# Routing search in four steps instead of six, one running sum instead of two, a new table of planner numbers and a branch hint

## The chip, the cores and the metric

The kernel runs on one core of a Trainium2 chip. The time is the device time in microseconds of one execution; three executions were timed before the change, and one more was profiled.

## The reference, cut to what matters

Attention over 8 batches, 8 heads, 576 tokens and 64 features keeps the 32 largest scores of each row. Its output, as 4608 tokens of 512 features, goes through 8 experts. Each token gets one expert, in the order of the logits, and no expert takes more than 576 tokens:

```
logits = x @ w_gate
flat = logits.flatten()
order = np.argsort(-flat)
...
for idx in order:
    tok, e = (int(idx) // E, int(idx) % E)
    if assigned[tok] >= 0 or counts[e] >= cap:
        continue
    assigned[tok] = e
...
    h = np.maximum(x[mask] @ w1[e], 0.0)
    out[mask] = h @ w2[e]
```

The inputs are fixed by their seed.

## The kernel before

The first part is attention. It writes `x` to DRAM and the logits `L` (128 partitions, 36 columns of 8 experts) to SBUF. The change leaves it alone. The second part, `moe`, runs the experts one after the other, in the order in which they fill up. For place p in that order there are five pieces.

`route` finds the expert that fills next. Each free token bids its largest logit for its best expert. In each of 6 steps VectorE compares all bids with 32 thresholds (`g`, L847) and TensorE counts, for each threshold and expert, the bids that lie above (`pc`, L851 for p = 0, L853 for the others). The highest threshold that some expert still fills 576 times becomes the lower end of the next step, with a spacing 32 times finer. For p = 0 a step has 36 small count matmuls; for p = 1 to 6 it has 9, and then two more matmuls (`tot`, L864, and `quart`, L867) with VectorE operations between them. The last expert needs no search. After the last step VectorE makes two masks: `M1` (L889) has the bids above the upper end of the last interval, `M2` (L890) has those within it. Each gets a running sum (`cs`, L900 and L901) and a sum over partitions on TensorE (L905 to L907), and they are joined to positions `pos` and a selection `sel` that is cut at 576 tokens.

`enlist` turns positions into a list of token numbers `idx` (L925 to L964). `weigh` reads the expert's number `ei` into a register of the SyncE queue (SP, L970), loads `w1` and `w2` in four pieces of 1 MB (`wr`, four buffers, L978), and splits each number into two float16 parts, on ScalarE (`w1h`, `w2h`, L990) and VectorE (`w1l`, `w2l`, L998). `bring` gathers the tokens by indirect DMAs of GpSimd (`xg`, L1020), five for each expert. For p = 0 TensorE turns them (L1033) and ScalarE and VectorE write the parts of `xT` (L1034, L1035); for the others VectorE and ScalarE make the parts first (L1043, L1046) and a transposing DMA of the SP queue turns them (L1047). `ffn` multiplies: 192 matmuls of `w1` (L1065), a ReLU in two parts `hh` and `hl` (L1084, L1085), 120 matmuls of `w2` (L1099, L1102), and a scatter of five tiles `ob` to the output (L1109 to L1114). The first four groups of p = 0 are cut, so that 128 columns can begin when the first gathered tile is there.

The order of all this isn't written out. `Plan` takes each operation with its engine, its cost, its predecessors and a due time, and simulates the engines: of what can begin soonest it emits that with the lowest due time. The table `O` in `moe` holds the numbers by which due times of the pieces are shifted, and windows for each engine. The emitted order is each engine's program, and an engine runs its program strictly in order. `stay` (L769) puts dummy matmuls into TensorE's gaps ahead of the first expert.

`verdict` checks that attention was exact and writes flags. At the end `redo` reads them on every engine (L629) and branches (L630): if one is set, faulty heads are computed again and `moe` is run again. Behind the branch stands the last scatter (L1175), of the last tile of the last expert.

Of the kernel before, what the change touches and what calls it, by code (L numbers as in the profile page):

```python
# [9 lines left out]
F32 = mybir.dt.float32  # L10
# [614 lines left out]
def redo(tc,q,k,v,w_gate,x,L,flags,again):  # L625
# [3 lines left out]
    any_=nc.values_load(flags[0:1,32:33],min_val=0,max_val=32)  # L629
    with tc.If(any_>0):  # L630
# [72 lines left out]
MT=32; MSTEPS=6  # L703
# [42 lines left out]
def moe(tc, K, L, x, w1, w2, out, tail, marks=None):  # L746
# [4 lines left out]
    T=MT; STEPS=MSTEPS; BIG=1e30; SX=128.0; SW=128.0; OSC=1.0/(SX*SW*SW)  # L751
    with ExitStack() as ctx:
# [6 lines left out]
        O=dict(WL1=-67.48, WL2=33.053, R1=216.021, XL=85.087, FA=-155.406, RT=5997.879, TE=0.633, TN=-42.68, WT=61.707, XT=21.675, RD=-5966.067, GL=2.3, W_V=0.109, W_A=0.0071, W_G=1000.0, W_P=0.0363, W_D=874040.4423, WD0=8.825, WD1=33.963, RA=16.129, WT0=-69.551, TE0=-175.381, XT0=-143.142, VD=228.308)  # L759
# [22 lines left out]
        U=cp.tile([128,NT],F32,name="U"); V.memset(U,1.0)  # L782
        stp=cp.tile([128,STEPS],F32,name="stp"); lo0=cp.tile([128,1],F32,name="lo0")
# [37 lines left out]
        def route(p,c):  # L821
# [13 lines left out]
            if p<E-1:  # L835
                pcs=3 if p==0 else GP; n=NT//pcs
                D_["lo"]=lo0; lowop=None
                for s in range(STEPS):
# [17 lines left out]
                    if p:  # L856
# [9 lines left out]
                        c.add("V",.07,lambda: V.tensor_scalar(o("ok",128,E,dt=BF16),D_["pn"][:,:E],float(CAP),-1.0/T,op0=ALU.is_ge,op1=ALU.add),k=0)  # L866
                        c.add("P",.04,lambda: P.matmul(D_["pn"][:,16:16+E],quart,D_["ok"],start=True,stop=True,skip_group_check=True))  # L867
# [19 lines left out]
                c.add("V",.3,high)  # L887
                c.add("V",.07,lambda: V.tensor_scalar(o("mem",128,NT),D_["ce"],D_["win"],None,op0=ALU.is_equal))
                c.add("V",.17,lambda: V.scalar_tensor_tensor(o("M1",128,NT),D_["v"],D_["hi"],D_["mem"],op0=ALU.is_ge,op1=ALU.mult))  # L889
                c.add("V",.17,lambda: V.scalar_tensor_tensor(o("M2",128,NT),D_["v"],D_["lo"],D_["mem"],op0=ALU.is_ge,op1=ALU.mult))  # L890
                c.add("V",.1,lambda: V.tensor_tensor(D_["M2"],D_["M2"],D_["M1"],op=ALU.subtract))
            else:
# [3 lines left out]
                def rest(): V.memset(o("M1",128,NT),0.0); V.tensor_copy(o("M2",128,NT),U)  # L896
                c.add("V",.2,rest)
            e["D"]=D_; e["ei"]=ei

            c.add("V",.17,lambda: V.tensor_tensor_scan(o("cs",128,2,NT)[:,0,:],onesf[:,:NT],D_["M1"],0.0,op0=ALU.mult,op1=ALU.add))  # L900
            c.add("V",.17,lambda: V.tensor_tensor_scan(D_["cs"][:,1,:],onesf[:,:NT],D_["M2"],0.0,op0=ALU.mult,op1=ALU.add))  # L901
            c.add("V",.07,lambda: V.tensor_copy(o("tot",128,2,dt=BF16),D_["cs"][:,:,NT-1]))
            def bases():
                pb=D_["pb"]=new(ps,[128,512],F32,"pc",1); tot=D_["tot"]
                P.matmul(pb[:,0:1],tri,tot[:,0:1],start=True,stop=True)  # L905
                P.matmul(pb[:,1:2],tri,tot[:,1:2],start=True,stop=False)
                P.matmul(pb[:,1:2],onesb,tot[:,0:1],start=False,stop=True)  # L907
            c.add("P",.08,bases)
            c.add("V",.07,lambda: V.tensor_copy(o("bs",128,2),D_["pb"][:,0:2]))
            c.add("V",.17,lambda: V.scalar_tensor_tensor(o("pos",128,NT),D_["cs"][:,0,:],D_["bs"][:,0:1],D_["M1"],op0=ALU.add,op1=ALU.mult))  # L910
            c.add("V",.17,lambda: V.scalar_tensor_tensor(o("p2",128,NT),D_["cs"][:,1,:],D_["bs"][:,1:2],D_["M2"],op0=ALU.add,op1=ALU.mult))
            c.add("V",.1,lambda: V.tensor_tensor(D_["pos"],D_["pos"],D_["p2"],op=ALU.add))
            c.add("V",.07,lambda: V.tensor_scalar(o("sel",128,NT),D_["pos"],0.5,None,op0=ALU.is_ge))
            e["sel"]=c.add("V",.1,lambda: V.scalar_tensor_tensor(D_["sel"],D_["pos"],float(CAP),D_["sel"],op0=ALU.is_le,op1=ALU.mult))
# [6 lines left out]
        def enlist(p,c):  # L921
# [3 lines left out]
            c.add("V",.07,lambda: V.tensor_scalar(o("pi",128,NT,dt=I32),D_["pos"],-1.0,None,op0=ALU.add))  # L925
# [8 lines left out]
            c.add("V",.15,lambda: V.tensor_tensor(tks,tk,D_["sel"].unsqueeze(1).to_broadcast([128,2,NT]),op=ALU.mult))  # L934
            last=[]
            for (u0,u1) in ((0,20),(20,36)):
                js=slice(u0,u1); n=u1-u0
# [265 lines left out]
```

## Time and profile before

| | |
|---|---|
| three timed executions | 1335.47 to 1340.48 us, median 1337.67 us |
| the profiled execution | 1336.32 us, of which the span of instructions is 1334.6 us |
| TensorE (PE) busy | 1228.7 us, 92% |
| VectorE (DVE) busy | 1143.0 us, 86% |
| ScalarE (ACT) busy | 953.5 us, 71% |
| GpSimd (POOL) busy | 831.8 us, 62% |
| granted TensorE clock | 0.979 of full speed in the mean |

Times in views of the trace are microseconds from the start of the span. Attention ends at about 868 us; the experts fill the rest. A busy share is a mean over stages that differ, so the stages of the second part are read one by one.

### The profile page before, as it was taken

The page shows a single profiled execution, that of the slowest core. Times are in us where ns is not written, and L with a number is a line of the kernel's source. Part 1 is how long each engine was busy: PE and PEld are TensorE (multiplying, and loading weights), DVE is VectorE, ACT ScalarE, POOL GpSimd, SP SyncE. Part 2 cuts the span into 40 slices and gives each one's busy share as a digit, 9 for nine tenths or more (in the row PEclk, how much of TensorE's full clock was granted, in tenths as well). Part 3 has the DMA queues.
Part 4 walks back from the last instruction along what each step waited for, and adds up shares of the span by engine and source line. Part 5 has one row for each costly group of instructions (what it writes and reads, how often), then busy time and mean ns, then how long its engine had stood idle before and what let it go on. Part 6 is the DMA issues. An engine that isn't in the chain of part 4 may idle for free.

```text
span 1334.6 us, 44588 instructions
## 1 busy us (share of the span) xinstructions
PE 1228.7 (92%) x16596; PEld 928.8 (70%) x16597; DVE 1143.0 (86%) x5729; ACT 953.5 (71%) x2241; POOL 831.8 (62%) x1219
## 2 busy tenths in 40 slices
PE   7999999999999999999999999838999999999996
PEld 6777777777777777777777777737565575665662
DVE  7989999999999899999999999579999898887520
ACT  4989999999999899999999999604433433433420
POOL 3888988988998899889889988701303203215101
PEclk9999999999999999999999999958999999999998
DMA  5544654654545545555554563013544644555601
GB/s 107 102 82 84 137 102 78 130 102 94 120 97 100 118 85 100 102 116 94 105 126 85 97 135 74 23 64 124 191 169 107 196 155 117 170 173 159 179 21 38
DMA packets 317973, 148.67 MB, mean 111 GB/s; under 512 B 283441, under 2 KB 299825, under 8 KB 316721
## 3 DMA queue, kind: packets, MB, share of 16 engines
q1 hardware_dynamic: 311408, 126.55, 42.4%
q0 software_dynamic: 5888, 18.88, 4.6%
q8 instruction: 132, 2.16, 0.7%
q14 instruction: 97, 0.79, 0.2%
q10 hardware_dynamic: 448, 0.30, 0.1%
HBM read 71.34 MB, written 18.87 MB: 68 GB/s over the span
## 4 chain that ended last, share of the span: by engine, by line
PE 29%; POOL 20%; ACT 18%; DVE 16%; issue 11%; DMA 5%; SPq 0%; POOLq 0%; ACTq 0%; another core or an unknown queue 0%; DVEq 0%
PE ph L1065 12%; POOL elm L456 10%; PE ph L1099 9%; DVE cd L371 6%; ACT w L385 6%; ACT F L450 4%; DMA Q<-nq 3%; POOL ehm L453 3%; ACT nq L309 2%; DVE st L398 2%; ACT r L403 2%; POOL e4l L509 2%; PE ph L1102 1%; PE s L367 1%; ACT st L381 1%
## 5 line engine op out<-in xcount | busy, mean ns | idle before, releaser
L371 DVE MAX8 cd<-s 128x8 f32<-128x96 f32 x1728 | 348.9, 248 | 10.8 <-PE s L367 10.3
L456 POOL TENSOR_TENSOR elm<-F,ehm 128x512 f16<-128x512 f32 x256 | 292.5, 1159 | 0.0
L398 DVE MAX8 st<-s 128x8 f32<-128x584 f32 x288 | 219.0, 770 | 9.6 <-PE s L388 5.9
L367 PE MATMUL s<-K,Q 128*128 128x192 f16 (+3 forms) x1280 | 197.5, 287 | 27.6 <-ACT r L403 9.0
L385 ACT ACTIVATE w<-s,st 128x576 uint16<-128x576 f32 x288 | 214.0, 743 | 8.3
L403 ACT ACTIVATE r<-s,st 128x576 bf16<-128x576 f32 x288 | 211.7, 746 | 0.6 <-DVE st L398 0.5
L1065 PE MATMUL ph<-xT,w1h 128*128 128x288 f16 (+2 forms) x1056 | 193.5, 283 | 0.4 <-DMA xT<-xs 0.4
L446 PE MATMUL pt<-Q,K 66*128 66x128 f16 (+1 forms) x1280 | 185.4, 215 | 0.9 <-DMA Q<-nq 0.8
L445 PE MATMUL pt<-Q,K 128*128 128x128 f16 (+1 forms) x1280 | 185.1, 214 | 0.0
L453 POOL TENSOR_SCALAR ehm<-F 128x512 f16<-128x512 f32 x256 | 156.4, 620 | 45.9 <-ACT F L450 45.9
L1114 POOL DMA_INDIRECT out_dram<-ob,idx x39 | 42.2, 1081 | 224.7 <-ACT ob L1109 203.7
L388 PE MATMUL s<-w,off 128*128 128x384 f16 x576 | 149.8, 284 | 20.3 <-ACT w L385 18.8
L450 ACT ACTIVATE F<-pt 128x512 f32<-128x512 f32 x256 | 153.3, 599 | 7.3 <-PE pt L446 4.1
L367 PEld LDWEIGHTS <-Q 128*128 128x128 f16 (+1 forms) x1280 | 99.9, 101 | 72.6 <-issue 61.8
L1065 PE MATMUL ph<-xT,w1l 128*128 128x288 f16 (+2 forms) x528 | 148.8, 283 | 0.0
L1020 POOL DMA_INDIRECT xg<-x,idx x40 | 44.2, 1106 | 144.4 <-DVE idx L964 60.3
L1084 ACT ACTIVATE hh<-ph 128x288 f16<-128x288 f32 x128 | 52.3, 410 | 113.3 <-PE ph L1065 96.7
L542 PE MATMUL pv<-vh,ehm 128*128 128x65 f16 x1024 | 119.8, 195 | 0.3 <-ACT F L450 0.3
L542 PE MATMUL pv<-vh,elm 128*128 128x65 f16 x1024 | 119.7, 193 | 0.4 <-POOL elm L456 0.4
L542 PE MATMUL pv<-vl,ehm 128*128 128x65 f16 x1024 | 119.9, 193 | 0.0
L446 PEld LDWEIGHTS <-K 66*128 66x128 f16 x1280 | 117.5, 98 | 2.1
L445 PEld LDWEIGHTS <-K 128*128 128x128 f16 x1280 | 117.0, 98 | 2.2 <-issue 1.8
(294 smaller groups left out, 3529.7 us busy)
## 6 DMA issues: line engine op xcount, KB each, us to landing
wr<-in_moe_w_dram SPq DMA_DIRECT2D x32, 1024.0 KB
kn<-in_k_dram SPq DMA_DIRECT2D x64, 128.0 KB
vt<-in_v_dram SPq DMA_DIRECT2D x64, 128.0 KB
x<-xb SPq DMA_DIRECT2D x8, 1024.0 KB
qn<-in_q_dram SPq DMA_DIRECT2D x62, 128.0 KB
Q<-nq SPq DMA_TRANSPOSE x160
kn<-in_k_dram SPq DMA_DIRECT2D x64, 16.0 KB
K<-nk SPq DMA_TRANSPOSE x64
```

Of the source, the lines that this page charges most:

```text
L367: x=T.matmul(s_ps[rows,S0+a:S0+b_],P[Q][:,qc],P[K][:,h*576+a:h*576+b_],start=(Q=="Q1"),stop=(Q=="Q2"))
L371: x=V.max(D["cd"][:,c*8:c*8+8],D["s"][:,S0+CW*c:S0+CW*(c+1)])
L385: A.activation(D["w"],D["s"][:,S0:S0+576],AF.Sign,bias=P["st"][:,i,32:33],scale=(1+2.0**-21),accum_out=acc[:,col])
L398: def next8(): V.max(P["st"][:,i,24:32],D["s"][:,S0-8:S0+576])
L403: A.activation(r,D["s"][:,S0:S0+576],AF.Relu,bias=P["st"][:,i,31:32],scale=-1.0)
L445: T.matmul(o,K2[:,kb:kb+128],Q1[:,qc],start=False,stop=False,skip_group_check=True)
L446: T.matmul(o,K3[0:66,kb:kb+128],Q2[0:66,qc],start=False,stop=(c==3 and h==sub[-1][0]),skip_group_check=True)
L450: A.activation(D["E"],D["pt"],AF.Exp,scale=ESC)
L453: G.tensor_scalar(D["eh"],D["E"],1.0,0.0,op0=ALU.mult,op1=ALU.add)
L456: G.tensor_tensor(el,D["E"],D["eh"],op=ALU.subtract); P["e"][i]=(D["eh"],el)
L542: for m_ in (range(N-3) if part==0 else range(N-3,N)): T.matmul(out,seq[m_][0],seq[m_][1],start=(m_==0),stop=(m_==N-1))
L1065: P.matmul(B["ph"][:,lo-c0:hi-c0],a[:,c,fs],xT[:,b+c,lo:hi],start=(i==0),stop=(i==11),skip_group_check=True)
```

## The change

`moe` takes a second number of steps: its first run (the one with `marks`) searches in 4 steps, the run inside `redo` in 6 as before. In the first run there is one mask, `sel`: the bids of the winning expert above the lower end. It gets one running sum, which begins at -1 so that it gives positions from 0 on, one sum over partitions, and one product to the integer positions `pi`; the cut at 576 is gone. In its place the last step keeps how many bids each threshold has above 575 (`ov`), sums over experts (`os`) and notes whether some threshold has a sum of exactly one (`one`), which is so when one expert has exactly 576 there and no other that many. `verdict` counts these notes and sets a further flag for each search that had none; then `redo` runs `moe` again with 6 steps.

For the planner, the load of a weight piece now costs 5.2 on the queue instead of 0.45, and all numbers of `O` are new. The product of token numbers and selection (`tks`) is due before the sums. At the end, the flags are read into registers before the last tile's `ob` is written, with a prefetch hint for the branch on ScalarE and GpSimd, and that write has to wait for the flags in the plan.

```diff
-MT=32; MSTEPS=6
+MT=32; MSTEPS=(6,4)
...
-    T=MT; STEPS=MSTEPS; BIG=1e30; SX=128.0; SW=128.0; OSC=1.0/(SX*SW*SW)
+    T=MT; STEPS=MSTEPS[1 if marks else 0]; BIG=1e30; SX=128.0; SW=128.0; OSC=1.0/(SX*SW*SW)
...
-        O=dict(WL1=-67.48, WL2=33.053, R1=216.021, XL=85.087, FA=-155.406, RT=5997.879, TE=0.633, TN=-42.68, WT=61.707, XT=21.675, RD=-5966.067, GL=2.3, W_V=0.109, W_A=0.0071, W_G=1000.0, W_P=0.0363, W_D=874040.4423, WD0=8.825, WD1=33.963, RA=16.129, WT0=-69.551, TE0=-175.381, XT0=-143.142, VD=228.308)
+        O=dict(FA=-381.864, GL=2.3, R1=211.263, RA=127.04, RD=-5914.06, RT=5987.22, TE=66.9612, TE0=-353.618, TN=-183.558, VD=361.245, WD0=43.2348, WD1=-15.6663, WL1=-283.997, WL2=71.1213, WT=-36.2651, WT0=18.9534, W_A=0.0415342, W_D=874040, W_G=1000, W_P=0.00439945, W_V=0.0355924, XL=25.6353, XT=45.8383, XT0=1.12987)
...
+                        if marks and s==STEPS-1: over=plan.at(c.t+.01,lambda: V.tensor_scalar(o("ov",128,E)[:T],D_["pn"][:T,:E],1.0-CAP,0.0,op0=ALU.add,op1=ALU.max),c.pre,e="V",d=.07,k=0)
...
-                def high():
-                    V.tensor_scalar(o("t1",128,1),D_["mx"],1.0,None,op0=ALU.add)
-                    V.scalar_tensor_tensor(o("hi",128,1),D_["t1"],stp[:,STEPS-1:STEPS],D_["lo_"],op0=ALU.mult,op1=ALU.add)
...
-                c.add("V",.17,lambda: V.scalar_tensor_tensor(o("M1",128,NT),D_["v"],D_["hi"],D_["mem"],op0=ALU.is_ge,op1=ALU.mult))
-                c.add("V",.17,lambda: V.scalar_tensor_tensor(o("M2",128,NT),D_["v"],D_["lo"],D_["mem"],op0=ALU.is_ge,op1=ALU.mult))
-                c.add("V",.1,lambda: V.tensor_tensor(D_["M2"],D_["M2"],D_["M1"],op=ALU.subtract))
+                if marks:
+                    r_=T if p==0 else 128
+                    n_=plan.at(c.t+2.0,lambda: V.tensor_reduce(o("os",128,1)[:r_],D_["ov"][:r_],axis=AX.X,op=ALU.add),[over],e="V",d=.07,k=0)
+                    e["one"]=plan.at(c.t+2.1,lambda: V.tensor_scalar(one[:r_,p:p+1],D_["os"][:r_],1.0,None,op0=ALU.is_equal),[n_],e="V",d=.07,k=0)
+                    c.add("V",.07,lambda: V.tensor_scalar(o("mem",128,NT),D_["ce"],D_["win"],None,op0=ALU.is_equal))
+                    e["sel"]=c.add("V",.17,lambda: V.scalar_tensor_tensor(o("sel",128,NT),D_["v"],D_["lo"],D_["mem"],op0=ALU.is_ge,op1=ALU.mult))
...
+            if marks:
+                c.add("V",.17,lambda: V.tensor_tensor_scan(o("cs",128,NT),onesf[:,:NT],D_["sel"],-1.0,op0=ALU.mult,op1=ALU.add))
+                c.add("V",.07,lambda: V.tensor_scalar(o("tot",128,1,dt=BF16),D_["cs"][:,NT-1:NT],1.0,None,op0=ALU.add))
+                def bases():
+                    D_["pb"]=new(ps,[128,512],F32,"pc",1); P.matmul(D_["pb"][:,0:1],tri,D_["tot"],start=True,stop=True)
+                c.add("P",.05,bases)
+                c.add("V",.07,lambda: V.tensor_copy(o("bs",128,1),D_["pb"][:,0:1]))
+                e["pos"]=c.add("V",.17,lambda: V.scalar_tensor_tensor(o("pi",128,NT,dt=I32),D_["cs"],D_["bs"],D_["sel"],op0=ALU.add,op1=ALU.mult))
...
-                ops.append(plan.at(c.t+.05*k,load,c.pre,take="wr",e="D",d=.45,late=2.0+3.0*(k+1),order=ops[-1:]))
+                ops.append(plan.at(c.t+.05*k,load,c.pre,take="wr",e="D",d=5.2,late=2.0,order=ops[-1:]))
...
+                    if marks and p==E-1 and j==3: tail["any"]=nc.values_load(marks[2][0:1,32:33],min_val=0,max_val=39); tc.mark_branch_hint_location("redo",hint=tail["any"],engines=[mybir.EngineType.Activation,mybir.EngineType.Pool])
...
+            c.add("V",.1,lambda: V.tensor_scalar(fl[:,npr:],R["pv"][:1,64:64+E-1],0.0,None,op0=ALU.is_equal))
```

The planner's order moves with it. Three places matter later.

On VectorE, ahead of the first part of `xT` for the first expert (L1035 before, L1055 now), the program read before:

```order
L832 TENSOR_REDUCE ce<-oh 128x36
L998 SCALAR_TENSOR_TENSOR w1l<-wr,w1h 128x512
L833 TENSOR_TENSOR ce<-ce,U 128x36
L998 SCALAR_TENSOR_TENSOR w2l<-wr,w2h 128x512
L834 TENSOR_TENSOR ohb<-ce,vb 128x288
L1035 SCALAR_TENSOR_TENSOR xT<-ph,xT 128x4x128
L847 TENSOR_TENSOR g<-v,vb 128x384 x2
```

and reads now, where L1018 is the weight split and L847 to L866 are the second expert's search:

```order
L834 TENSOR_TENSOR ohb<-ce,vb 128x288
L847 TENSOR_TENSOR g<-v,vb 128x384 x2
L880 TENSOR_SCALAR base<-iTs,lo_23856 128x32
L847 TENSOR_TENSOR g<-v,vb 128x384
L1018 SCALAR_TENSOR_TENSOR w1l<-wr,w1h 128x512
L857 TENSOR_TENSOR cm<-pc,dm 128x32
L1018 SCALAR_TENSOR_TENSOR w1l<-wr,w1h 128x512
L860 TENSOR_REDUCE ch<-cm 128x8
L1018 SCALAR_TENSOR_TENSOR w1l<-wr,w1h 128x512
L866 TENSOR_SCALAR ok<-pc 128x8
L1055 SCALAR_TENSOR_TENSOR xT<-ph,xT 128x4x128
L1018 SCALAR_TENSOR_TENSOR w1l<-wr,w1h 128x512
```

A whole comparison step of the second expert's search, and three splits of `w1`, moved in front of the first `xT`, and one split of `w1` still stands behind it; before, all eight splits of `w1` and one of `w2` stood in front of it. Counted from `idx` on, 21 instructions of VectorE stand ahead of that `xT` now, seven of them splits of `w1`; before there were 15, seven of them splits too (six of `w1`, one of `w2`).

On TensorE, the first matmuls of the first expert stood behind the second turned tile; there the program read before:

```order
L769 LDWEIGHTS tri
L769 MATMUL ph<-tri 128x128
L1033 MATMUL ph<-identm,xg 128x128 x4
L1065 LDWEIGHTS w1h
L1065 MATMUL ph<-xT,w1h 128x128
```

and now there is this around the second turned tile, where L768 is the dummy matmul and L868 the last matmul of a search step:

```order
L768 LDWEIGHTS tri
L768 MATMUL ph<-tri 128x128
L1053 MATMUL ph<-identm,xg 128x128 x4
L868 LDWEIGHTS quart
L868 MATMUL pc<-ok,quart 128x8
```

and, five dummies later, this around the third, where L1085 is the matmul of `w1`:

```order
L768 LDWEIGHTS tri
L768 MATMUL ph<-tri 128x128
L1053 MATMUL ph<-identm,xg 128x128 x4
L1085 LDWEIGHTS w1h
L1085 MATMUL ph<-xT,w1h 128x128
```

The third turned tile (`xg`, L1053) and a whole step of the second expert's search stand ahead of the first matmul of `w1` now; two turned tiles instead of three come behind it. Between the end of the first search and that matmul there were 92 dummies and there are 77.

On the SP queue, in the middle of the experts, before:

```order
L978 DMA wr<-in_moe_w_dram 128x4x512
L1047 DMA_TRANSPOSE xT<-xs 128x8x128 x4
L1047 DMA_TRANSPOSE xT<-xs 128x8x64
L970 TENSOR_LOAD ei
```

and now:

```order
L998 DMA wr<-in_moe_w_dram 128x4x512
L1067 DMA_TRANSPOSE xT<-xs 128x8x128 x3
L990 TENSOR_LOAD ei
L990 ISA x2
L1067 DMA_TRANSPOSE xT<-xs 128x8x128
L998 ISA
L998 DMA wr<-in_moe_w_dram 128x2x1024
L1067 DMA_TRANSPOSE xT<-xs 128x8x64
```

The read of the next expert's number (`ei`), which waits for a search on VectorE, and a load of weights, which waits for a buffer, stand between the transposes of one expert now; before, a transpose stood behind its own expert's loads alone.

## Rows read from the trace of the kernel before

**Rows 1.** Windows: stretch; busy us of PE, PEld, DVE, ACT, POOL; clock; DMA share, GB/s.

```profile
920.00:930.00 10.00, 10.00 (x103) 8.58 (x101) 8.81 (x29) 3.26 (x8) 0.00 (x0) 0.85 0.01 2
...
970.00:980.00 10.00, 8.77 (x84) 6.18 (x84) 9.93 (x30) 2.84 (x7) 1.21 (x1) 1.00 0.31 79
...
1250.00:1300.00 50.00, 50.00 (x333) 31.25 (x332) 13.98 (x29) 11.45 (x26) 4.82 (x5) 1.00 0.10 33
```

**Rows 2.** The chain that ended last: start, us, what; two steps of the first search.

```profile
882.83 1.43 PE pc L851 x36
...
885.79 1.43 PE pc L851 x36
```

**Rows 3.** VectorE's timeline (start, us, what) in the first search step.

```profile
875.32 1.48 DVE L847 TENSOR_TENSOR g<-v,vb 128x384 bf16<-128x384 f32 x3
...
877.16 0.90 DVE L817 TENSOR_SCALAR stp<-stp 128x1 f32<-128x1 f32 x5
```

**Rows 4.** The chain after the first search: first and last of twelve pieces.

```profile
894.37 0.07 DVE t L885
...
897.59 0.10 DVE pi L925
```

**Rows 5.** The chain at the end of the first list.

```profile
901.89 1.49 PE ph L769 x14
...
905.52 0.17 DVE idx L964
```

**Rows 6.** VectorE's timeline between the first list and the first matmul of `w1`.

```profile
907.64 0.68 DVE L998 SCALAR_TENSOR_TENSOR w1l<-wr,w1h 128x512 f16<-128x512 f32 x1
...
908.61 0.68 DVE L998 SCALAR_TENSOR_TENSOR w1l<-wr,w1h 128x512 f16<-128x512 f32 x1
...
912.21 0.68 DVE L1035 SCALAR_TENSOR_TENSOR xT<-ph,xT 128x512 f16<-128x512 f32 x1
```

**Rows 7.** TensorE's timeline: the third turned tile, and the fourth with its wait.

```profile
916.00 0.63 PE L1033 MATMUL ph<-identm,xg 128*128 128x128 f32 x4
...
918.66 0.63 PE L1033 MATMUL ph<-identm,xg 128*128 128x128 f32 x4 [1.92 <-issue]
```

**Rows 8.** The chain at the first matmul of `w1`.

```profile
913.21 0.50 PE ph L1065 x9
```

**Rows 9.** The chain further on: runs of one kind of matmul.

```profile
1007.86 2.71 PE ph L1102 x24
...
1135.70 0.07 PE pc L853 x3
...
1143.38 8.47 PE ph L1065 x69
...
1251.83 10.37 PE ph L1099 x48
```

**Rows 10.** TensorE's waits from 913 to 1323 us: in total, times, longest.

```profile
PE pc L867 <- DVE ok L866: 3.8, 5, 1.0
PE ph L1033 <- issue: 1.9, 1, 1.9
PE pc L853 <- DVE g L847: 1.6, 3, 0.8
```

**Rows 11.** ScalarE's timeline: the last tile.

```profile
1322.46 0.60 ACT L1109 ACTIVATE ob<-ph 128x512 f32<-128x512 f32 x1 [4.53 <-PE ph L1099]
```

**Rows 12.** GpSimd's timeline: the last two scatters.

```profile
1318.20 0.96 POOL L1114 DMA_INDIRECT out_dram<-ob,idx  x1 [3.71 <-ACT ob L1109]
1326.14 0.96 POOL L1175 DMA_INDIRECT out_dram<-ob,idx  x1 [6.97 <-ACTq L630]
```

**Rows 13.** The chain at the end.

```profile
1318.20 4.71 DMA out_dram<-ob,idx
...
1323.07 1.70 another core or an unknown queue
...
1325.24 0.04 POOLq L1175
```

More of the change, by code (lines that the diff above doesn't have):

```diff
@@ L782, in moe @@
         U=cp.tile([128,NT],F32,name="U"); V.memset(U,1.0)
+        one=cp.tile([128,E],F32,name="one"); G.memset(one,0.0)
         stp=cp.tile([128,STEPS],F32,name="stp"); lo0=cp.tile([128,1],F32,name="lo0")
@@ L901, in route @@
[L901 to L907, printed above, removed]
@@ L933, in enlist @@
             c.add("V",.1,lambda: V.scalar_tensor_tensor(D_["qf"][:,1],D_["qf"][:,1],5.0,D_["qf"][:,2],op0=ALU.mult,op1=ALU.add))
-            c.add("V",.15,lambda: V.tensor_tensor(tks,tk,D_["sel"].unsqueeze(1).to_broadcast([128,2,NT]),op=ALU.mult))
+            mt=plan.at(c.t if marks else c.t+.05,lambda: V.tensor_tensor(tks,tk,D_["sel"].unsqueeze(1).to_broadcast([128,2,NT]),op=ALU.mult),[e["sel"],X[p-1]["idx"] if p else None],e="V",d=.15,k=0)
             last=[]
@@ L943, in enlist @@
                 ga=plan.at(c.t+.01,fa,c.pre,e="V" if AHV else "G",d=.07+n*32*.00104 if AHV else 1.2,w=c.w,k=0)
[L944 removed]
+                for i in range(2): c.add("V",.07+n*20*.00104,lambda js=js,i=i,n=n: V.tensor_tensor(D_["bt"][:,js,i],D_["bh"][:,js],tks[:,i,js].unsqueeze(2).to_broadcast([128,n,20]),op=ALU.mult),mt,k=0)
                 cv=c.pre
@@ L1119, in verdict @@
             n9=acc.shape[1]; npr=n9//9
-            c_,r,ok,good,want,bad,nf,fl=(cp.tile(z,F32,name=n_) for z,n_ in (([128,n9],"vc"),([128,n9],"vr"),([128,n9],"vok"),([128,npr+4],"good"),([1,npr+4],"want"),([1,npr+4],"bad"),([1,1],"nf"),([1,npr],"flf")))
+            c_,r,ok,good,want,bad,nf,fl=(cp.tile(z,F32,name=n_) for z,n_ in (([128,n9],"vc"),([128,n9],"vr"),([128,n9],"vok"),([128,npr+4],"good"),([1,npr+4],"want"),([1,npr+4],"bad"),([1,1],"nf"),([1,npr+E-1],"flf")))
             c.add("V",.36,lambda: V.tensor_scalar(c_,acc,-0.5,-256.0,op0=ALU.mult,op1=ALU.add))
@@ L1136, in total @@
             def total():
-                D_=R["pv"]=bank(); P.matmul(D_[:1,:npr+1],onesf[:,0:1],good[:,:npr+1],start=True,stop=True)
-            tv=c.add("P",.11,total,take="ph",m=1)
+                D_=R["pv"]=bank(); P.matmul(D_[:1,:npr+1],onesf[:,0:1],good[:,:npr+1],start=True,stop=True); P.matmul(D_[:1,64:64+E-1],onesf[:,0:1],one[:,:E-1],start=True,stop=True)
+            tv=c.add("P",.16,total,*[X[p]["one"] for p in range(E-1)],take="ph",m=1)
+            c.add("V",.1,lambda: V.tensor_scalar(fl[:,npr:],R["pv"][:1,64:64+E-1],0.0,None,op0=ALU.is_equal))
             c.add("V",.1,lambda: V.tensor_tensor(bad[:,:npr+1],want[:,:npr+1],R["pv"][:1,:npr+1],op=ALU.subtract),free=[tv])
             c.add("V",.1,lambda: V.tensor_scalar(bad[:,:npr],bad[:,:npr],bad[:,npr:npr+1],None,op0=ALU.add))
-            c.add("V",.1,lambda: V.tensor_scalar(fl,bad[:,:npr],0.0,None,op0=ALU.not_equal))
+            c.add("V",.1,lambda: V.tensor_scalar(fl[:,:npr],bad[:,:npr],0.0,None,op0=ALU.not_equal))
             c.add("V",.1,lambda: V.tensor_reduce(nf,fl,axis=AX.X,op=ALU.add))
             c.add("V",.07,lambda: V.tensor_copy(flags[:,npr:npr+1],nf))
-            c.add("V",.07,lambda: V.tensor_copy(flags[:,0:npr],fl))
+            R["flags"]=c.add("V",.07,lambda: V.tensor_copy(flags[:,0:npr],fl[:,:npr]))
         X=[{} for _ in range(E)]
@@ L1150, in moe @@
             route(p,c)
-            enlist(p,Chain(c.t+(TE if p else TE0),X[p]["sel"],X[p-1]["idx"] if p else None,w=0.0 if p else PW))
+            enlist(p,Chain(c.t+(TE if p else TE0),X[p]["pos"],X[p-1]["idx"] if p else None,w=0.0 if p else PW))
             weigh(p,p*47.0-(WT if p else WT0))
```

56 lines of the change are left out of this document (36 added, 20 removed).

## The prediction

> **What bounds the kernel now.** Attention isn't touched, so the experts' part alone is read, from 868 us on. First come the windows of granted clock and busy time: TensorE is busy all through 920 to 930 and 1250 to 1300 us, and in 970 to 980 us it is idle for 1.2 us while VectorE is busy for 9.93 of 10 [rows 1]. So once the first expert's matmuls run, TensorE is the bound nearly everywhere, VectorE stands close behind it in the early experts, and falls to 14 of 50 us at the end. The reader is to see three stages: a serial one, in which the first expert is searched and nothing multiplies; a long one, in which TensorE's program sets the end; and a tail behind the last matmul.
>
> The chain of waits tells what the serial stage is made of. Two count groups of the first search lie 885.79 - 882.83 = 2.96 us apart [rows 2]: that is one step of six. The first list `idx` is done at 905.52 + 0.17 = 905.69 [rows 5], and the first matmul of `w1` comes at 913.21 [rows 8], 7.52 behind it. From there to the last tile's activation at 1322.46 [rows 11] is 409.3 us. The experts' own matmuls cost, by runs without a gap, 192 x 8.47/69 = 23.57 for `w1` and 96 x 10.37/48 = 20.74 plus 2.71 for `w2` [rows 9], so 47.0 for one expert and 376.2 for eight. The remaining 33 us are searches, lists, turned tiles, waits and a low clock; of these and of the serial stage the change can take something.
>
> **The serial stage.** Two steps less: 2 x 2.96 = 5.9. In the first step VectorE makes five spacings in 0.90 us [rows 3], now three: 0.4. Behind the search twelve pieces go: `t1`, `hi`, one mask, the subtraction, one running sum, two matmuls, `p2`, the sum to `pos`, two pieces of `sel`, and `pi`, which the product now writes; they run from 0.03 to 0.22 us and sum to 1.76 [rows 4]. Added are `ov`, `os` and `one`; `ov` and `os` lie where VectorE waits for TensorE anyway, and if it didn't, three pieces of 0.1 would cost 0.3; I take 0.1. `tks`, `w8c` and the penalty now stand among the sum's pieces: between 0 and 0.5, I take 0.3. So 1.76 - 0.4 = 1.4. Between the two halves of the list's matmuls stood 14 dummies of 1.49 us [rows 5], now two: between 0 and 1.28, since VectorE's products for the second half run meanwhile; I take 0.6. One split of `w1`, 0.6 long, no longer stands ahead of `idx`: between 0 and 0.6, I take 0.3. In sum `idx` comes 5.9 + 0.4 + 1.4 + 0.6 + 0.3 = 8.6 earlier, at about 897.1.
>
> Not all of that reaches the first matmul, which needs the first `xT` and all eight splits of `w1`. In the new order VectorE does a whole comparison of the second search in front of that `xT`: three `g` of together 1.48 [rows 3] and four small ones of some 0.1, less the 0.1 of `U`. Ahead of the matmul there are also eight splits instead of seven; two splits with one other operation between them start 0.97 apart [rows 6], of which 0.6 is the split. The way from `idx` grows by 1.48 + 0.3 + 0.6 = 2.4, to 9.9, and the matmul comes 8.6 - 2.4 = 6.2 earlier. TensorE has a gate of its own: the third turned tile now stands ahead. It ran at 916.00 before, 10.3 behind `idx`, and took 0.63 [rows 7]. If the gather's arrival set that, the first matmul is only 8.6 - (10.9 - 7.5) = 5.2 earlier. The program order spoke against an arrival that late, as the tile stood behind 48 matmuls of `w1` there. I take **6.0**, with 8.6 and 4 as ends; 4 is for gathers that now fall into the weight loads.
>
> **TensorE's program.** Six searches lose two steps: 12 x 9 counts at 0.07/3 [rows 9] and 24 small matmuls at about the same, 3.1; of the sum's matmuls 14 go, at 0.03: 0.4. **3.5**, rather firm, as TensorE never has room to hide them.
>
> Its waits for VectorE within searches are 3.8 and 1.6 us [rows 10]. A third of the steps goes and a third of that with them, 1.8. VectorE also has less to do: each step costs it 1.48 for `g` and some 0.8 around it, so 12 steps take 28 us off it, in the experts where it is full. For the other two thirds of the waits I take half, 1.8 again: **3.6**, between 0 and 5.4.
>
> In the first expert TensorE waited 1.9 us at the fourth turned tile [rows 7, 10], and behind that the granted clock was 0.85 in 920 to 930 [rows 1]: 15% of the stretch at the lower of its two levels (1.2 GHz), as the mean of a level of 0.5 and one of 1.0, is 3 us at half speed, so 1.5 lost. Now two turned tiles come later than the first matmul, in a program that has 48 short matmuls of 128 columns first; I take the wait as gone and half of the clock's loss, 1.9 + 0.7 = **2.6**, between 0 and 3.4. The third turned tile costs its **0.6** in the wait ahead of the first matmul instead of behind it.
>
> The new numbers of `O` and the load's cost of 5.2 add no instruction. What they move is priced above where a row shows it; elsewhere, with nothing to price it, zero, and the two rivals below for the loss. The extra operations of `verdict` lie where VectorE is idle for 36 of 50 us [rows 1].
>
> **The tail.** ScalarE writes the last tile until 1322.46 + 0.60 = 1323.06 [rows 11], and the scatter that needs it starts at 1326.14, released by ScalarE's queue at the branch [rows 12]: 3.1 us. With the register loaded and the branch hinted before, ScalarE may release it at once. But GpSimd has its own business there: the scatter before lands at 1318.20 + 4.71 = 1322.91, then 1.70 us pass, and its queue is through at 1325.28 [rows 13]. The hint takes away none of that, so the scatter can't start before about 1325.3: **0.9**, between 0 and 3.1.
>
> The Trainium skill (Runtime: NRT & Kernel Launch, Instruction fetch mechanics) says that a taken branch to a page that isn't among the fetched ones stops the engine until a DMA has brought that page. By that rule a hint on both engines would take all 3.1 us, and the sum would be 2.2 lower.
>
> **The sum.** 6.0 + 3.5 + 3.6 + 2.6 + 0.6 + 0.9 = 17.2. The profiled execution took 1336.3, so 1319.1; the median of the runs is 1.35 above it, so **1320.5 us**. All good ends together (8.6, 3.5, 5.4, 3.4, 0.6, 3.1) give 24.6, so 1313; the bad ends (4, 3.5, 0, a loss of 1.5 for the clock, 0.6, 0) 6.6, so 1331.
>
> **Rivals.**
> 1. *The branch is the whole tail.* GpSimd's 1.70 us would be part of its own branch and go with the hint. For it: nothing in the chain names that time. Against it: it begins only when the scatter before has landed. 1320.5 - 2.2 = 1318.3. This is what the skill's rule would give.
> 2. *New waits eat the gain.* The planner's order is a guess of what runs when; on the SP queue the read of the next `ei` and a load now stand between one expert's transposes. Both wait, for a search and for a buffer, and the transposes behind them wait too, and then TensorE. For it: VectorE, which makes all of these, is full early on [rows 1]. Against it: the weights are asked for earlier than before. At 1.5 us for each of six experts it is 9 us: 1329.5, or 1324 to 1336 around it.
> 3. *The clock falls.* Between the search and the first matmul there are 77 dummies instead of 92, thinly spread at the end. If TensorE starts the matmuls at the lower level twice as long as in rows 1, 3 us are lost where 0.7 were gained: 1324.2.
> 4. *Slower.* The same place as in 2, but a transpose is held until whole search steps have run. To end 0.5% slower than before, 17.2 + 6.7 = 24 us have to come back, 4 us for each of six experts. Two outstanding steps of the first search's length would be 5.9 each, 35 us: 1356. Against it: searches have a third fewer steps and, in the new program, lie a whole expert ahead of their use.
> 5. *The search isn't exact.* Then the experts run twice, some 466 us more. Worked out on the reference's inputs, a search with 32 thresholds and 4 steps ends at exactly 576 tokens in each of the seven searches.
>
> **How the numbers follow.** Forecast 0.59, rival 1 0.13, rival 2 0.14, rival 3 0.08, rival 4 0.05, rival 5 0.01. The range of 1313 to 1331 holds nearly all of the forecast, of rivals 1 and 3 and half of rival 2: some 0.85. A measurement of this kernel tells about 0.5% from no change, 6.7 us, so faster means below 1331.0: forecast, rivals 1 and 3 and half of rival 2, 0.87; the same 0.07; slower 0.06.
>
> **What would show it.** The first search: four count groups 2.96 apart. The first matmul of `w1` about 6 us earlier, near 907, behind the third turned tile. From it to the last activation about 399 us instead of 409.3, with TensorE's waits for `ok` and `g` under 3 us together and no wait of 1.9 at a turned tile. The last scatter 2.2 behind the last tile instead of 3.1. The prediction is wrong if TensorE's waits name the transposes or `xs`, if the clock is low behind the first matmul, or if the way from `idx` to it is longer than 11 us.

## The result, and the profile after

| | before | changed |
|---|---|---|
| timed executions beside each other | 1335.47 to 1340.65 us, median 1339.08 | 1321.64 to 1325.61 us, median 1324.39 |
| ratio, 95% interval | | 0.988 (0.986 to 0.990) |
| the same in a later set of runs | median 1342.31 us | median 1323.78 us, 0.986 (0.983 to 0.989) |
| profiled execution, span | 1334.6 us | 1323.9 us |

The change takes 14.7 us off the median, 1.1% (1.2% by the ratio). The prediction was 1320.5 us, 17.2 off the profiled execution.

The chain of waits of the changed kernel (start, us, what) from the first search to the first `xT`:

```profile
882.64 1.42 PE pc L851 x36
885.60 1.43 PE pc L851 x36
888.56 1.42 PE pc L851 x36
...
900.28 0.04 DVE idx L984
...
901.48 6.34 DMA xg<-x,idx
...
910.65 0.19 DVE cm L857
```

The steps are 2.96 us apart, as in [rows 2]. But a transfer of 6.34 us now stands on the chain behind `idx`: the first gather of tokens. VectorE's timeline in that stretch, with the first instruction of the experts on top (in brackets the idle time ahead of an instruction and what ended it):

```profile
873.48 0.45 DVE L790 TENSOR_REDUCE rng<-L 128x1 f32<-128x288 f32 x1 [1.24 <-DMA x<-xr]
...
900.28 0.17 DVE L984 SCALAR_TENSOR_TENSOR idx<-f 128x5 int32<-128x5 f32 x1
...
906.85 0.69 DVE L1018 SCALAR_TENSOR_TENSOR w1l<-wr,w1h 128x512 f16<-128x512 f32 x1
910.65 0.19 DVE L857 TENSOR_TENSOR cm<-pc,dm 128x32 f32<-128x32 f32 x1 [3.11 <-PE pc L853]
...
912.15 0.68 DVE L1055 SCALAR_TENSOR_TENSOR xT<-ph,xT 128x512 f16<-128x512 f32 x1
```

And TensorE's:

```profile
907.87 1.12 PE L1053 MATMUL ph<-identm,xg 128*128 128x128 f32 x4 [3.84 <-DMA xg<-x,idx]
...
910.33 0.29 PE L853 MATMUL pc<-ohb,g 128*128 128x32 bf16 x3
...
912.58 0.60 PE L1053 MATMUL ph<-identm,xg 128*128 128x128 f32 x4
913.02 0.28 PE L1085 MATMUL ph<-xT,w1h 128*128 128x128 f16 x2
```

The reader is to see one wait handed on: the gather is late, the first turned tile waits 3.84 us for it, the counts of the second search stand behind that tile, and VectorE, whose `cm` needs the counts, waits 3.11 us with splits of `w1` and the first `xT` queued behind.

TensorE's waits from then to the end of the program (total, times, longest):

```profile
PE ph L1053 <- DMA xg<-x,idx: 3.8, 1, 3.8
PE pl L979 <- DVE o L975: 1.3, 1, 1.3
PE pl L968 <- DVE bt L964: 1.1, 1, 1.1
PE pc L915 <- DVE tot L913: 1.0, 1, 1.0
PE pc L853 <- DVE xs L1066: 0.9, 1, 0.9
PE pc L853 <- DVE g L847: 0.7, 1, 0.7
PE pl L968 <- issue: 0.5, 1, 0.5
PE pc L868 <- DVE ov L867: 0.2, 1, 0.2
```

The waits for `ok` and `g` of [rows 10] have shrunk from 5.4 to 0.9 us (0.7 for `g`, and 0.2 ahead of L868, which the view puts down to `ov`), and the 1.9 us at a turned tile is gone. Waits within the lists (`o`, `bt`, `tot`) are new, as are one of 0.9 us behind `xs` and one of 0.5 that the view can't name: 4.8 us together. The windows (columns as in [rows 1]) show the clock at its full level, 1.00, where it was 0.85:

```profile
920.00:930.00 10.00, 10.00 (x107) 8.15 (x105) 10.00 (x32) 3.98 (x9) 0.00 (x0) 1.00 0.01 2
...
1250.00:1300.00 50.00, 50.00 (x338) 30.75 (x338) 9.07 (x24) 10.15 (x22) 5.46 (x6) 1.00 0.07 24
```

The second window can't be compared with that of before as it stands, since it lies 10.7 us nearer to the last tile. Counted back from that tile, VectorE is busy for 9.1 of the last 50 us now and was for 8.0, so it does not have less to do there.

The tail: ScalarE's last tile, then GpSimd's last two scatters, each from its timeline.

```profile
1311.74 0.60 ACT L1130 ACTIVATE ob<-ph 128x512 f32<-128x512 f32 x1 [4.53 <-PE ph L1119]
```

```profile
1307.48 0.97 POOL L1135 DMA_INDIRECT out_dram<-ob,idx  x1 [3.71 <-ACT ob L1130]
1315.45 0.96 POOL L1197 DMA_INDIRECT out_dram<-ob,idx  x1 [7.01 <-issue]
```

The last scatter is 3.1 us behind the tile, exactly as in [rows 11, 12].

**Where the time went.** Attention, which nothing touched, ended 2.9 us later in this profile than in that of before (873.48 against 870.58), so stretches are counted from VectorE's first instruction of the experts (`rng`). All profiled runs, in us (the stretch "to the last tile" runs from the first matmul of `w1` to the start of ScalarE's last tile, the tail from that tile's end to the start of the last scatter; expectations below that speak of "attention's end" count from 0.3 us earlier):

| profiled run | `rng` starts | to `idx` | `idx` to first `w1` | to the last tile | tail | from `rng` to the span's end |
|---|---|---|---|---|---|---|
| before | 870.58 | 35.1 | 7.4 | 409.4 | 3.1 | 464.0 |
| changed | 873.48 | 27.0 | 12.6 | 398.7 | 3.1 | 450.4 |
| changed, again | 873.27 | 27.0 | 13.7 | 396.0 | 3.1 | 448.8 |
| no hint | 870.18 | 27.0 | 12.5 | 397.8 | 2.5 | 448.9 |
| scatter first | 871.19 | 27.0 | 13.0 | 397.2 | 0.3 | 450.8 |
| counts first | 869.02 | 27.0 | 9.4 | 396.0 | 2.9 | 444.3 |
| counts first, again | 874.69 | 27.0 | 9.4 | 397.3 | 2.9 | 445.5 |
| hold | 872.70 | 27.0 | 9.4 | 396.2 | 2.6 | 444.1 |
| hold, again | 871.96 | 27.0 | 9.6 | 398.3 | 2.8 | 446.7 |
| hold, turned tile pinned first | 871.30 | 27.0 | 9.4 | 399.1 | 2.9 | 447.3 |
| all mends | 872.32 | 27.0 | 9.5 | 399.9 | 0.3 | 449.8 |
| new table, old load cost | 873.23 | 27.5 | 10.0 | 399.6 | 2.6 | 448.6 |
| new table, six steps | 872.95 | 33.3 | 11.0 | 409.9 | 3.0 | 466.1 |
| old table, four steps | 870.12 | 27.2 | 10.0 | 415.2 | 2.9 | 464.3 |

Of the 13.6 us between the first two rows, 8.1 come from the list, 5.2 are given back on the way to the first matmul, 10.7 come from the stretch of matmuls, and nothing from the tail.

### The profile page after: what moved, and what is told of

The parts are those of the page before. It is cut to its first block, busy times and chain, and to the rows that moved or that the text cites. A ratio compares the mean times of both kernels' runs of the same rounds, so it can differ in the third digit from the quotient of the medians.

```text
span 1323.9 us, 43963 instructions
## 1 busy us (share of the span) xinstructions
PE 1219.8 (92%) x16361; PEld 922.1 (70%) x16362; DVE 1095.1 (83%) x5536; ACT 950.3 (72%) x2241; POOL 828.1 (63%) x1220
## 4 chain that ended last, share of the span: by engine, by line
POOL 20%; DVE 20%; ACT 19%; PE 18%; issue 15%; DMA 6%; SPq 1%; POOLq 0%; another core or an unknown queue 0%; ACTq 0%; DVEq 0%
POOL elm L456 10%; ACT w L385 7%; PE ph L1085 7%; DVE cd L371 6%; PE ph L1119 5%; ACT F L450 4%; DMA Q<-nq 3%; POOL ehm L453 3%; DVE st L398 2%; ACT nq L309 2%; ACT r L403 2%; POOL e4l L509 2%; DMA xg<-x,idx 1%; PE s L367 1%; DVE g L847 1%
## 5 line engine op out<-in xcount | busy, mean ns | idle before, releaser
L1085 PE MATMUL ph<-xT,w1h 128*128 128x288 f16 (+2 forms) x1056 | 191.1, 282 | 0.1
L1135 POOL DMA_INDIRECT out_dram<-ob,idx x39 | 38.7, 993 | 201.7 <-ACT ob L1130 177.1
L1085 PE MATMUL ph<-xT,w1l 128*128 128x288 f16 (+2 forms) x528 | 148.0, 282 | 0.0
```

What stands on the lines that cost most here:

```text
L1085: P.matmul(B["ph"][:,lo-c0:hi-c0],a[:,c,fs],xT[:,b+c,lo:hi],start=(i==0),stop=(i==11),skip_group_check=True)
```

## The experiments

**The tail: no hint** (one run).

```diff
-...; tc.mark_branch_hint_location("redo",hint=tail["any"],engines=[mybir.EngineType.Activation,mybir.EngineType.Pool])
```

> The prefetch hint on ScalarE and GpSimd is left out; the flags are still read into registers before the last tile. Theory: the hint does nothing here, since the last scatter waits for GpSimd's own queue, which waits for the landing of the scatter before it and then 1.7 us more. So the last scatter starts 3.1 us behind the end of the last tile's activation, as in the kernel before (3.08) and in the changed one (3.11), and ScalarE still has some 2.5 us between its branch and its next instruction. Rival: the hint does shorten the branch, and the changed kernel would have been slower in the tail without it: the distance grows to 4 us or more.

The scatter came 2.5 us behind the tile, a little sooner than in the changed kernel (3.1); other runs with the hint give 2.6 to 3.1. The 0.6 us are those of the scatter before, which landed 4.26 us after its start here and 4.85 there. From GpSimd's timeline of this run:

```profile
1310.64 0.96 POOL L1197 DMA_INDIRECT out_dram<-ob,idx  x1 [6.42 <-ACTq L629]
```

The hint is worth nothing here. The trace's events at the branch say more (us; "next" is the first instruction of the engine behind it):

| engine, run | hint | branch | next, behind the branch |
|---|---|---|---|
| GpSimd, changed | 1308.12 | 1308.22 | 2.4 |
| GpSimd, no hint | | 1303.90 | 2.6 |
| GpSimd, scatter first | 1304.83 | 1309.08 | 0.5 |
| ScalarE, changed | 1307.18 | 1311.74 | 2.5 |
| ScalarE, no hint | | 1307.52 | 2.6 |

On GpSimd the hint stood 0.1 us ahead of its branch. With 4.3 us between them, in the next experiment, the branch took 0.5 us instead of 2.4. The Trainium skill (Runtime: NRT & Kernel Launch, Instruction fetch mechanics) has a taken branch whose target isn't among the fetched pages wait until a DMA has brought it; GpSimd agrees with that, in one run. The packets of the instruction queue, 16 KB each, fit: in the changed kernel one starts at 1309.54, behind GpSimd's branch, and one at 1313.32, behind ScalarE's; in the next experiment one starts at 1306.24, behind GpSimd's hint and ahead of its branch, and one at 1309.98, again behind ScalarE's branch (1308.45). Which engine a packet is for isn't recorded. So the hint seems to have brought GpSimd's target early and not ScalarE's, whose 2.5 us stayed in place with 4.6 us of lead; why is open. None of it sets the end, though. GpSimd is idle behind its branch until the scatter before has landed. The chain of the changed kernel:

```profile
1307.48 4.85 DMA out_dram<-ob,idx
...
1312.48 1.71 another core or an unknown queue
...
1314.66 0.04 POOLq L1197
1314.71 0.52 issue
```

**The tail: the last scatter ahead of the branch** (timed).

```diff
-                if p<E-1 or j!=3: plan.at(t2+i_*.64+.2,scatter,[a],...)
+                plan.at(t2+i_*.64+.2,scatter,[a],...)
...
-        tc.nc.gpsimd.indirect_dma_start(out=out, ..., in_=tail["ob"], in_offset=None)
```

> The last scatter is issued where the others are, ahead of the branch, and the one behind the branch is gone (the second run inside the branch writes its own). Theory: GpSimd's business at the branch is what the last scatter waits for; ahead of it the scatter starts about 0.7 us behind the end of the last activation instead of 2.5 to 3.1, and what GpSimd does behind its last scatter keeps its 8.4 us: the kernel ends 2.0 to 2.4 us earlier than the changed one. Rival: the wait for the landing and the 1.7 us behind it only change places with the scatter and come behind it; then 8.4 grows to 10.5 or more and the time is unchanged.

GpSimd's timeline has the last scatter 0.3 us behind the tile (ScalarE wrote it from 1308.44 for 0.60):

```profile
1304.18 0.96 POOL L1135 DMA_INDIRECT out_dram<-ob,idx  x1 [3.71 <-ACT ob L1130]
1309.32 0.96 POOL L1135 DMA_INDIRECT out_dram<-ob,idx  x1 [4.17 <-ACT ob L1130]
```

But from there to the span's end (1321.9) it takes 12.6 us instead of 8.4, so the kernel ends 12.9 us behind the tile instead of 11.5: the rival, and worse than it said. The median of 1318.92 (0.986 of before, 0.982 to 0.989) can't be told from the changed kernel's.

**The start: counts first.** One order added for the planner: the first turned tile comes behind the counts of the second search's first step. Ahead of the branch, VectorE's program is the same instruction for instruction.

```diff
...
+        X[0]["turn0"]["order"].append(X[1]["first"]); X[0]["turn0"]["n"]+=1; X[1]["first"]["next"].append(X[0]["turn0"])
```

> In TensorE's program the first count group of the second search stands ahead of the first turned tile instead of behind it; VectorE's program is the same. Theory A (order): VectorE waited 3.1 us for these counts while they stood behind a tile that waited for its gather; with the wait gone it does its weight splits meanwhile, and the first matmul of w1 comes 10.4 us behind the first list instead of 12.6. Theory B (the gather alone): VectorE's wait was hidden behind the late gather anyway, or the third turned tile is the gate; the distance stays above 12. Under both, the first gather lands 7.4 us behind the list, as in the changed kernel.

TensorE's timeline of this run:

```profile
901.47 0.24 PE L853 MATMUL pc<-ohb,g 128*128 128x32 bf16 x3 [1.29 <-DVE g L847]
...
902.54 0.24 PE L853 MATMUL pc<-ohb,g 128*128 128x32 bf16 x3 [0.25 <-DVE g L847]
...
903.32 0.66 PE L1054 MATMUL ph<-identm,xg 128*128 128x128 f32 x4 [0.53 <-DMA xg<-x,idx]
...
905.41 0.28 PE L1087 MATMUL ph<-xT,w1h 128*128 128x128 f16 x2
```

`idx` was done at 896.01 here, so the gather is as late as before (7.3 behind it), but the first matmul comes 9.4 behind it instead of 12.6: 3.2 us, and 1 more than theory A said. The wait of VectorE behind the counts was the whole of what the way had too much.

**The start: w2 loads held** (one run). A transfer of 16 bytes on SP reads the first gathered tile, and stands ahead of the first expert's two `w2` loads.

```diff
...
+                if p==0 and k==2:
+                    def hold(): S.dma_start(out=new(sm,[1,4],F32,"hold",1),in_=e["xgs"][0][0:1,0:4])
...
+                if p==0 and j==0: h=e["hold"]; h["pre"].append(g); h["n"]+=1; g["next"].append(h)
...
```

> The two loads of w2 for the first expert stand behind a small transfer that reads the first gathered tile, so they start when it has landed; and the counts stand ahead of the first turned tile, as in the run with that alone. Theory (the gather is slowed by the weight loads beside it): the first gather lands about 5 us behind the list instead of 7.4, and the first matmul of w1 comes 9.5 us behind it, about 1 us sooner than by the order alone. Rival: the gather takes its 6.3 us with no loads beside it too; then it lands at 7.4 and nothing is gained over the order alone. If the later w2 loads hurt, the stretch from the first matmul to the last activation grows from 398.7 by a us or more.

In the program that ran the counts were not ahead: the order line of counts first wasn't in it, and with the hold alone the planner kept the turned tile first. So this run is the hold by itself. TensorE's timeline:

```profile
904.30 0.66 PE L1057 MATMUL ph<-identm,xg 128*128 128x128 f32 x4 [1.34 <-DMA xg<-x,idx]
905.35 0.23 PE L853 MATMUL pc<-ohb,g 128*128 128x32 bf16 x3
...
909.03 0.28 PE L1089 MATMUL ph<-xT,w1h 128*128 128x128 f16 x2
```

and the gather on its chain:

```profile
900.69 3.56 DMA xg<-x,idx
```

3.56 us instead of 6.34: the loads beside it cost the gather 2.8 us. Windows of the transfers agree: in the changed kernel the 16 DMA engines were busy with a share of 1.06 in 900 to 905 us, at 394 GB/s; here with 0.36, at 97 GB/s. First the changed kernel, then the hold (columns as in [rows 1]):

```profile
900.00:905.00 5.00, 4.03 (x40) 3.85 (x37) 4.82 (x13) 1.06 (x1) 2.91 (x3) 0.62 1.06 394
```

```profile
900.00:905.00 5.00, 3.66 (x40) 3.48 (x38) 4.93 (x13) 0.49 (x2) 3.39 (x4) 0.76 0.36 97
```

The Trainium skill (DMA: Bandwidth & Descriptors, Queues, rings and completion order) has each DMA engine take packets in turn from the queues that have work. By that rule a gather among loads waits for their packets, and the trace agrees. The first matmul comes 9.4 us behind the list again.

**The same with the turned tile pinned ahead of the counts** (one run; the order line of counts first, turned round).

> The same hold of the two w2 loads, with TensorE's first turned tile ahead of the counts as in the changed kernel. Theory: the gather lands about 5 us behind the list, the turned tile is done before the comparison of the second search is, the wait of VectorE for the counts shrinks from 3.1 to under 1 us, and the first matmul of w1 comes about 9.5 to 10 us behind the list: either mend alone is worth 2 to 3 us, and both together little more than one. Rival: order and gather add, and this run stays 1.5 us or more behind the one with both.

9.4 once more, as its order at the start is the same as that of the hold alone. Whether order and gather add, its rival's question, is settled by the next run.

**All mends: counts first, hold, scatter ahead of the branch** (timed).

> Counts of the second search ahead of the first turned tile, the w2 loads of the first expert held until the first gather has landed, and the last scatter ahead of the branch. Theory: counts and hold each alone brought the first matmul to 9.4 us behind the list, where VectorE's own program is the gate (the comparison ends 7.0 behind the list), so both together give 9.2 to 9.4, not 6; the stretch to the last activation is about 396 as with each, and the tail 2 us shorter if the scatter run shows that: from attention's end to the end 442 to 445 us, 6 to 8 less than the changed kernel. Rival: order and gather add, and the first matmul comes at 8 or less.

9.5: order and gather don't add. In every one of these runs `cm` comes 7.0 to 7.2 us behind the list, where VectorE's own comparison is done, and the first matmul 2.4 later. The rest of the total was missed: the stretch was 399.9, and the scatter ahead of the branch gained 2.6 us ahead of itself and lost 4.2 behind. Median 1318.94, 0.985 of before (0.982 to 0.989).

**Steps and table apart: six steps with the new table** (timed).

```diff
-MT=32; MSTEPS=(6,4)
+MT=32; MSTEPS=(6,6)
```

> The first run searches in 6 steps again; the single mask and sum, the flags, the new table of planner numbers, the load cost and the hint stay. Theory (the steps and the sum carry the gain, the table nothing): the first list comes 5.9 + 0.3 later than in the changed kernel, the first matmul stays 12.5 us behind it, and the stretch from that matmul to the last activation grows from 398.7 by 3.1 for the counts and 2 to 4 for waits: from attention's end to the end 461 to 464 us instead of 450.7, so no better than 0.3% under the kernel before. Rival (the new table carries the stretch): the stretch stays below 402, and from attention's end to the end it is under 458.

Slower than before: 1340.64, 1.0028 (1.0012 to 1.0043). The stretch of matmuls is 409.9 and the way from `rng` to the end 466.1, both beyond what theory or rival said; the first matmul came 11.0 behind the list, not 12.5. TensorE's waits in it:

```profile
PE ph L1085 <- DMA xT<-xs: 4.5, 2, 3.8
PE pc L853 <- DVE g L847: 4.5, 5, 3.1
```

**Four steps with the old table and the old load cost** (timed).

```diff
-        O=dict(FA=-381.864, GL=2.3, R1=211.263, ...)
+        O=dict(WL1=-67.48, WL2=33.053, R1=216.021, ...)
...
-                ops.append(plan.at(c.t+.05*k,load,c.pre,take="wr",e="D",d=5.2,late=2.0,order=ops[-1:]))
+                ops.append(plan.at(c.t+.05*k,load,c.pre,take="wr",e="D",d=.45,late=2.0+3.0*(k+1),order=ops[-1:]))
```

> The old table of planner numbers and the old load cost of 0.45, with four steps, one sum, flags and hint as in the changed kernel. Theory (the table gives nothing and costs at the start): the first list comes 27 to 28 us behind attention's end, the first matmul 7.4 us behind the list as in the kernel before, and the stretch from it to the last activation is 409.4 less 3.5 for matmuls and 3.6 for waits, about 402; from attention's end to the end 449 us, 1 to 2 less than the changed kernel. Rival: the old table with shorter searches makes TensorE wait in other places, as its due times were set for six steps; the stretch stays above 406, and the whole at 453 or more.

The rival held: 1331.61, 0.9954 (0.9931 to 0.9976), with executions from 1326.5 to 1336.1; the profiled one was the slowest, 4.5 us above the median, and what follows is read from it alone. Its waits of TensorE and, under them, what held VectorE:

```profile
PE pc L864 <- DVE ch L860: 12.4, 4, 7.8
...
PE ph L1053 <- issue: 1.9, 1, 1.9
```

```profile
1120.27 0.68 DVE L1066 SCALAR_TENSOR_TENSOR xs<-xg,xs 64x512 f16<-64x512 f32 x1 [7.69 <-ACT xs L1063]
1120.88 0.18 DVE L857 TENSOR_TENSOR cm<-pc,dm 128x32 f32<-128x32 f32 x1
```

The last tokens' `xs` stands in the middle of a search step. Its gather was issued at 1106.76 among weight loads and ScalarE could start at 1119.61. `cm`, `ch` and the matmul L864 stand behind it in their programs, so TensorE stands too. The changed kernel has a gather as slow at about that time, and its chain shows it:

```profile
1107.10 10.74 DMA xg<-x,idx
```

but there the search of that time had ended at 1106 us, ahead of `xs`; what stands behind `xs` is the end of a list, and TensorE's wait for it is the 1.3 us for `o`.

**New table with the old load cost** (timed).

```diff
-..., d=5.2,late=2.0,order=ops[-1:]))
+..., d=.45,late=2.0+3.0*(k+1),order=ops[-1:]))
```

> The new table of planner numbers with the old load cost of 0.45. In the planned order the first matmul of w1 stands behind the second turned tile again and no comparison of the second search ahead of the first part of xT, as in the kernel before; so the order at the start comes from the load cost, not from the table. Theory (table and load cost only work together): the first matmul comes 9.5 to 10 us behind the list, as with the old table, and TensorE's waits in the experts come back: the stretch is 404 or more, and from attention's end to the end 453 or more. Rival (the table alone carries the stretch): it stays under 400, and with the earlier first matmul the whole is 2 to 3 us under the changed kernel.

The way is 10.0, as expected, with the order of before at the start. But the stretch stays at 399.6: the rival, except that from `rng` to the end it is only 0 to 2 us less. Median 1323.84, 0.987 (0.983 to 0.990), the same as the changed kernel's 1323.78 in the set of runs below. So it is the table, not the load cost, that four steps need.

**The changed kernel and two mends, timed beside each other.**

> The changed kernel once more, unchanged, timed beside the next two on one chip. If the lag of 2.9 us at attention's end in its first profile was a spread between executions, attention ends elsewhere here (868 to 873 us in the runs so far), while the first list comes again 27.3 us behind it, the first matmul of w1 12.5 to 13.0 behind the list, and the stretch to the last activation is 397 to 399: from attention's end to the end 449 to 451 us. If it belonged to the change, attention ends at 873 again.

> Counts of the second search ahead of the first turned tile, nothing else, now timed. In the one look the stretch from attention's end to the end was 444.6 us, against 450.7 and 449.2 in two looks at the changed program: 3.1 at the first matmul, which should return exactly, and 2 to 3 later, which may be spread. Theory: 3 to 6 us under the changed kernel on the same chip, 1.2 to 1.6% under the kernel before. Rival: what the first matmul gains is given back at the wait for the slow gather near 1110 us, and the medians agree within 1 us.

> The w2 loads of the first expert held behind the first gathered tile, timed. The earlier look under the name with counts first was this same program: only the hold is in it, and the turned tile still stands ahead of the counts; what was expected there of both holds for the run with all mends. Theory: as in that look the first gather lands 4.6 us behind the list and the first matmul 9.4; 3 to 6 us under the changed kernel, no different from counts first. Rival: the later w2 loads push against the second expert's, and it is 1 to 3 us behind counts first.

| | median | ratio to before |
|---|---|---|
| changed | 1323.78 us | 0.9861 (0.9832 to 0.9890) |
| counts first | 1323.36 us | 0.9853 (0.9822 to 0.9885) |
| hold | 1320.87 us | 0.9837 (0.9810 to 0.9864) |

By time, counts first can't be told from the changed kernel: the medians are 0.4 us apart, within the 1 us that its rival gave, and its executions scatter from 1315.79 to 1326.11. The hold can: each of its six (1316.89 to 1321.33) is shorter than each of the changed kernel's five (1321.92 to 1324.90), and the medians are 2.9 us apart. The intervals against the kernel before hide that, as its executions vary by 11.6 us.

Attention ended again at 873.27 in the changed kernel, which by the expectation's rule would speak for the change; but counts first, which has the same attention program, ended it at 869.02 in one run and 874.69 in the other. It is a spread between executions, and larger than what is asked for. From `rng` to the end the profiled runs part: 444.1 to 447.3 us with either mend alone (five runs), 448.8 to 450.4 with the changed kernel's order and tail (three runs, one of them without the hint). The 3 us or more at the first matmul stand in every one of them. That they are kept to the end is shown by time for the hold alone; for counts first it stays open, and with all mends the stretch took them back.

## Why the prediction was right, and where it was not

**The list.** Predicted 8.6 us earlier; it was 35.1 - 27.0 = 8.1. Steps 2.96 apart, as said.

**The way to the first matmul.** Predicted to grow from 7.5 to 9.9; it grew to 12.6 and 13.7. So the start gave 2.9 and 1.8 us instead of 6.0, below the low end of 4. The prediction had called itself wrong if this way came out longer than 11 us; here it was. The step that failed: "The way from `idx` grows by 1.48 + 0.3 + 0.6". It priced a piece of VectorE's program by the durations of its instructions. One of them, `cm`, needs counts from TensorE, and those stood behind a turned tile that waits for a gather. As a price of VectorE's own list it was right: with the counts moved, or the gather sped up, the way is 9.4. The slowed gather was named as the reason for the low end of 4, and then left with too little weight: it took 6.34 us instead of 3.95, and its 2.4 us went onto the path by way of the counts, which the prediction had put beside it. The 3.95 are read from the kernel before, from the gather's start on GpSimd to the end of TensorE's wait, 0.05 ahead of the first turned tile as in the changed kernel:

```profile
906.80 1.60 POOL L1020 DMA_INDIRECT xg<-x,idx  x1 [43.11 <-DVE ml L826]
```

```profile
910.80 0.65 PE L1033 MATMUL ph<-identm,xg 128*128 128x128 f32 x4 [2.70 <-DMA xg<-x,idx]
```

**TensorE's stretch.** Predicted 3.5 + 3.6 + 2.6 + 0.6 = 10.3 less; it was 10.7, and 13.4 in the second profiled run. Taking for each kind of matmul (line and shape) the median distance from its start to the next one's as its price, the stretch has 391.2 us of price and 17.8 beyond it before, 386.7 and 11.6 now: 4.5 for matmuls (said: 4.1) and 6.2 for waits and clock (said: 3.6 + 2.6). The signs came too: `ok` and `g` under 1 us together, no 1.9 us, a clock of 1.00 in 920 to 930 us. But that 6.2 meets 6.2 is luck in part. By the view of waits, `ok` and `g` lost 4.5 us and the turned tile 1.9, more than was said, and 4.8 us of waits came that the prediction put at nothing; with the smaller ones the view's total fell from 8.0 to 5.7 only (3.8 in the second run). The rest is the clock and distances too short for that view.

**Its reason was half of it.** The prediction put the waits down to fewer steps and gave the new numbers of `O` zero. Six steps with the new table have 19.4 us beyond the price, four steps with the old table 27.3 (in its slowest execution), both together 11.6. By the ratios, steps and sum alone are worth 0.5%, table and sum alone cost 0.3%, and together they are worth 1.2%. With the old table, a gather's consumer stands within a search step; with six steps and the new table, TensorE waits for `xT` and `g`. Why the planner's order comes out so for these numbers isn't shown. "Elsewhere, with nothing to price it, zero" was the step: the table had no price of its own, yet the gain from the steps hung on it.

**The tail.** Predicted 0.9, measured 0. The row that it went by [rows 13] has GpSimd's queue through at 1325.28, and [rows 12] the scatter at 1326.14; those 0.9 us lie between the queue's last step and any scatter's start (1314.70 and 1315.45 now), and were taken for ScalarE's doing. GpSimd alone sets the tail, with and without a hint.

**The rivals.** Rival 1 failed: with the hint the tail is the 3.1 us of before. No wait for the transposes or `xs` of any size but 0.9, so rival 2 failed here, though a wait for `xs` was one of the signs that the prediction gave against itself; it came true in the run with six steps, where TensorE waits 4.5 us for `xT`. The clock stayed up (rival 3). No search was inexact: the experts ran once. In sum 17.2 was predicted; 13.6 came in the first profiled run, 15.2 in the second, 14.7 in the medians. The start fell 3 to 4 us short and the tail 1; the list and the stretch carry the result.

## What to carry to other kernels

Where one engine's program is priced piece by piece, look through each piece for what it needs from another engine, and read in that engine's order what stands ahead of it: a list of short instructions can hold a transfer. Planner numbers and algorithm are one change: the shorter search paid fully only with due times made for it. When a stage that nothing touched varies by more than the effect, compare profiled runs from a common instruction on as well as whole times.

## What the runs showed of the hardware

A gather of 128 rows of 2 KB took 3.56 us with the loads held (97 GB/s moved in that stretch), 3.95 with the loads running out (272 GB/s), 6.34 among loads (394 GB/s), and 10.74 and 12.05 near 1100 us, where scatters run as well (in the changed kernel and with counts first). The same attention program ended between 869.0 and 874.7 us. A scatter put ahead of the branch started 2.8 us sooner behind its tile, and the kernel ended 1.4 us later behind it: the last thing that GpSimd does, a drain, took 6.6 us although its last transfer had landed, and 7.8 us before, where the transfer lay within it. A branch of GpSimd took 0.5 us when its hint was 4.3 us ahead, 2.4 when it was 0.1 ahead and 2.6 without one; on ScalarE 4.6 us ahead changed nothing.
